# Linear attention, gated MLP and MLP in one launch: side jobs held back during a value product, one low half put out earlier

## The chip, the cores and the metric

The program runs on one core of a Trainium2 chip. The metric is the device time of one execution in microseconds (us). Five engines work side by side: PE multiplies matrices (PEld loads its weights), DVE and POOL do element-wise arithmetic, ACT does activations and copies, SP issues DMAs. POOL issues DMAs too.

## What is computed

```python
def _attn_ref(q, k, v, omega):            # 4 x 8 heads, 576 tokens, head_dim 64, 128 features
    scale = 1.0 / np.sqrt(np.sqrt(D))
    def phi(x):
        h = x @ omega.T - sum(x * x) / 2
        return np.exp(h - max(h)) / np.sqrt(m)
    kv = phi(k).T @ v;  z = sum(phi(k))
    return (phi(q) @ kv) / (phi(q) @ z + 1e-6)

def _moe_ref(x, w_gate, w_val, w_out, rms_g):   # 2304 tokens, d_model 512, d_ff 1536
    xn = x / rms(x) * rms_g
    return (silu(xn @ w_gate) * (xn @ w_val)) @ w_out

def _moe2_ref(x, w_in, w_out):                  # d_ff 2048
    return silu(x @ w_in) @ w_out

out = _moe2_ref(_moe_ref(_attn_ref(q, k, v, omega), ...), ...)
```

(The reference's formulas in short form: phi is applied to scaled q and k, and rms is the root mean square over d_model.) All of it is float32, and the weights reach the kernel as 64-bit numbers.

## The kernel before, in words

**Arithmetic.** A float32 factor is held as two fp32r tiles: a high half (an ACT copy that rounds) and a low half (DVE: the number minus its high half). Each product is three matmul passes: high by high, high by low, low by high (`PASS`). For activations that is `split_h`: L198 on ACT makes "h high", L199 on DVE makes "h low". For weights it is L468 (ACT) and L472 (DVE).

**Tokens.** The 2304 tokens stand in five blocks j = 0 to 4: four of 512 and one of 256. d_model is cut into four pieces d (KC = 4) of 128 rows.

**Weights.** A weight tile of 128 x 512 arrives as two 32-bit words (`raw`). Five DVE instructions (L146 to L157) and two POOL adds (L160) make a float of them ("decoding"); for the gate and value weights ACT scales by the RMS gain (L168, four instructions); then L468 and L472 split.

**Phases.** The first 205 us or so are the attention, with the first two f (pieces of 128 of d_ff) of the gated MLP for blocks 0 to 2 mixed in. Then `stream` sets the order: blocks 3 and 4 of those two f, then the *third f* for all five blocks in the order j = 1, 0, 2, 3, 4. For one block, `g1_glu` multiplies by the gate weights ("g", L205), applies silu (L227), puts the previous block's output products (`mid`, "y", L272, made by `g2_glu`) in between, multiplies by the value weights ("v", L205), multiplies both (DVE, L233) and splits the result into h. `g2_glu` makes y in four pieces d; in the third f these go through staging tiles, copied by ACT (L284) two pieces to a tile, to DRAM by an adding DMA that POOL issues (L288), and a staging tile is only free again when its DMA has landed. In the last GLU step each piece is instead added to ya (DVE, L294), copied to its high half (ACT, L296), and `low(d)` (L262) makes its low half one piece later; `low` of the last piece came after the loop's last yield.

After the third f come GLU units u = 0 to 8, one f each, and then units of the second MLP, two f each. `quad` runs a unit's input product for blocks 0 to 3 with seven products in place of eight; it needs sums and differences of tokens (`token_sums`: L398, L401 on DVE, split by L390 on ACT and L393 on DVE) and of weights (tile `ws`, L367 on POOL, split by L468 and L472; they are the keys ("s", u, 0) and ("s", u, 1), and the jobs `slo(0)` and `slo(1)` make their low halves). In `quad`, L607 are the input products, L619 and L634 ACT's silu and copies, L639 a DVE addition of two partial products, L701 and L715 the DVE products before h is split. `glu_block` (L738, L741) does block 4. In the first MLP unit `mlp_block` and `g1_mlp` work without `quad`.

**What sets the order.** The program is written out by one driver loop. `stream` yields the cost of each piece of PE work, and the loop puts side jobs between them:

```python
        for c in stream():
            due += c
            gone = gone + c if sums or ... else 0.0
            if sums and gone > wq.rest:
                sums.pop(0)()
                gone = ...
            if wq.hold:
                due = min(due, M_PACE)
            elif due > wq.pace and wq.tick():
                due = min(due - wq.pace, wq.pace)
```

`sums` is the list of token-sum jobs, one being written out each `wq.rest` of PE work; `wq.tick` writes out the next weight job (a decoding step, a split, a sum of weights) each `wq.pace`. Where a job stands in an engine's instruction order is therefore where it waits: each engine executes its own list in order.

Of the kernel before, what the change touches and what calls it, by code (L numbers as in the profile page):

```python
# [20 lines left out]
def kernel(  # L21
# [22 lines left out]
    KC = DM // P  # L44
# [177 lines left out]
    def g1_glu(f, j, hs, mid):  # L222
        wq.need((1, "g", f))
        p = ps_tile("ps_g" if blocks[j] == TB * P else "ps_y", [P, blocks[j]])
        yield from proj2(wt[1, "g", f], j, p)
        s = pools["s"][0].tile([P, blocks[j]], F32, tag="s", name="s", bufs=pools["s"][1])
        nc.scalar.activation(out=s, in_=p, func=AF.Silu)  # L227
        if blocks[j] == TB * P:
            yield from mid
        wq.need((1, "v", f))  # L230
        p = ps_tile("ps_g" if blocks[j] == TB * P else "ps_y", [P, blocks[j]])
        yield from proj2(wt[1, "v", f], j, p)
        nc.vector.tensor_tensor(out=s, in0=s, in1=p, op=ALU.mult)  # L233
        if mid is None:
            wait.append(lambda: hs.update({f: split_h(s, j)}))
            return
        hs[f] = split_h(s, j)
        if blocks[j] < TB * P:
            yield from mid
# [15 lines left out]
    def g2_glu(fs, j, hs, first, last, calm=False):  # L255
        wq.need(*[(1, "o", f) for f in fs])
        staged = j < NE and not last
        y = ya[j].rearrange("p (c t) -> p c t", c=KC)
        nn = 3 * len(fs)

        def low(d):
            (nc.gpsimd if 0 < j < NE else nc.vector).tensor_tensor(  # L262
                out=xs[j][:, 1, d, :], in0=y[:, d, :],
                in1=xs[j][:, 0, d, :].bitcast(F32), op=ALU.subtract,
            )

        for d in range(KC):
            ps = ps_tile("ps_y", [P, blocks[j]])
            n = 0
            for f in fs:  # L270
                for a, c in PASS:
                    nc.tensor.matmul(  # L272
                        out=ps,
                        lhsT=wt[1, "o", f][:, a, d * P:(d + 1) * P],
                        rhs=hs[f][:, c, :],
                        start=(n == 0),
                        stop=(n == nn - 1),
                    )
                    n += 1
            if staged:  # L280
                if d % 2 == 0:
                    o = stage()
                if d % 2 == 0 or calm:
                    nc.scalar.activation(out=o[:, d % 2, :], in_=ps, func=AF.Copy)  # L284
                else:
                    nc.vector.tensor_copy(out=o[:, 1, :], in_=ps)
                if d % 2:
                    nc.gpsimd.dma_start(  # L288
                        out=kept(j, d // 2), in_=o.rearrange("p t d -> p (t d)"), accum_op=ALU.add
                    )  # L290
            elif first:
                nc.scalar.activation(out=y[:, d, :], in_=ps, func=AF.Copy)
            else:
                nc.vector.tensor_tensor(out=y[:, d, :], in0=ps, in1=y[:, d, :], op=ALU.add)  # L294
            if last:
                nc.scalar.activation(out=xs[j][:, 0, d, :], in_=y[:, d, :], func=AF.Copy)  # L296
                if d:
                    low(d - 1)
            yield nn * blocks[j] / 2365
        if last:  # L300
            low(KC - 1)

    def out_pair(j, n):
        i = j * TB + 2 * n
# [118 lines left out]

    class WeightQueue:
        def __init__(self):
            self.jobs, self.st, self.hold, self.free, self.held, self.tail, self.pace, self.rest = [], {}, True, [], {}, [], A_PACE, T_PACE
            for u in range(len(groups)):
                self.plan(u)

# [318 lines left out]
        else:  # L748
            wait.append(lambda: hs.update({f: split_h(s, j)}))

    def mlp_block(f, j, hs, ys, n):
        wq.need((2, "i", f))
        p = ps_tile("ps_g", [P, blocks[j]])
        for k in range(2):
            yield 3 * KH * blocks[j] / 2365
            part(wt[2, "i", f], j, p, 3 * KH * k, 3 * KH * (k + 1))
            yield from take(ys, n[k])
        s = pools["s"][0].tile([P, blocks[j]], F32, tag="s", name="s", bufs=pools["s"][1])
        nc.scalar.activation(out=s, in_=p, func=AF.Silu)
        hs[f] = split_h(s, j)  # L760

    def take(ys, n):
        for _ in range(n):
# [4 lines left out]
    def flush():  # L768
        while wait:
            wait.pop(0)()  # L770
        yield from ()
# [5 lines left out]
    def stream():  # L777
# [27 lines left out]
        for n, (j, fs) in enumerate(order):  # L805
# [4 lines left out]
            if n == 1:  # L810
# [2 lines left out]
                    wq.slot(("t", k), F32)  # L813
                now, later23 = sums23()
                sums.extend(now)
                wq.rest = 2.0
            if n == 2:
                sums[:0] = later
                wq.free += [(0, 4), (0, 5)]
# [6 lines left out]
        for u, (kind, fs) in enumerate(groups):  # L826
# [6 lines left out]
            if std <= u < std + NSTD:  # L833
# [7 lines left out]
                for n, k in enumerate(each):  # L841
# [4 lines left out]
                            ys = chain_of(ys, out_of(1))  # L846
                        wq.release(*wq.keys(u - 1)[1])
                    j = 3 - n // 2 if first else 1 - n // 2
                    yield from mlp_block(fs[n % 2], j, hs[j], ys, k if n < 3 else (k[0], 9))
                wq.hold = False  # L850
                if first:
                    assert wq.jobs.pop(0)[0] == 1 << 10
# [762 lines left out]
    with tc.manual_schedule():  # L1615
# [68 lines left out]
        for c in stream():  # L1684
            due += c
            gone = gone + c if sums or wq.rest in (T_PACE, M_PACE + T_PACE) else 0.0
            if sums and gone > wq.rest:
                sums.pop(0)()
                gone = gone - wq.rest if wq.rest not in (T_PACE, M_PACE + T_PACE) else 0.0
# [34 lines left out]
```

## Time and profile before

| | us |
|---|---|
| three runs | 946.83, 951.12, 951.9 (median 951.12) |
| the profiled execution, its own time | 951.37 |
| its span in the profile | 949.6 |
| PE busy | 929.1 (98%) |
| DVE busy | 709.4 (75%) |
| ACT busy | 530.7 (56%) |
| POOL busy | 477.5 (50%) |

The page's chain that ended last is 86% PE, 7% DVE, 3% ACT. A timeline row of one engine gives the start in us from the start of the span, the time it took, engine and line, operation, destination and source, how many instructions it stands for, and in brackets how long the engine sat idle before it and which instruction or DMA ended that. PEclk in the windows is the granted clock of TensorE as a share of full speed.

### The profile page before, as it was taken

The numbers are of one execution on the slowest core, as the hardware profiler recorded it, in microseconds if no ns is written. First come the engines' busy times: TensorE is split into PE (matmuls) and PEld (weight loads), VectorE is DVE, ScalarE is ACT, GpSimd is POOL, SyncE is SP. The second block draws the span as 40 slices with busy tenths as digits, with TensorE's granted clock in tenths as the row PEclk, the third lists the DMA queues.
The fourth block names the chain that finished last, engine by engine and source line by source line (L and its number), as shares of the span: only waits on it lengthen the run. The fifth ranks groups of instructions, "written<-read, shape, count | busy, mean of one in ns | idle before, by whom it ended". The sixth has DMA issues, their size and how long they took to land.

```text
span 949.6 us, 17368 instructions
## 1 busy us (share of the span) xinstructions
PE 929.1 (98%) x6480; PEld 776.0 (82%) x6480; DVE 709.4 (75%) x1323; ACT 530.7 (56%) x1157; POOL 477.5 (50%) x495
## 2 busy tenths in 40 slices
PE   8999999997999999999999999999999999999998
PEld 6888878885878888888888877888888888888886
DVE  6998999866777867877787888978675757575633
ACT  6999977644455355454445445556444454545442
POOL 8888655005435645545454554465554545454411
PEclk9999999999999999999999999999999999999999
DMA  7655543306347658658657740646878787878777
GB/s 187 171 135 146 139 127 101 144 25 143 78 89 158 139 103 181 134 105 180 144 100 156 177 156 3 215 117 136 161 130 170 129 164 136 158 147 148 116 147 166
DMA packets 98788, 129.65 MB, mean 137 GB/s; under 512 B 29456, under 2 KB 75792, under 8 KB 98704
## 3 DMA queue, kind: packets, MB, share of 16 engines
q0 software_dynamic: 17280, 59.78, 36.4%
q1 hardware_dynamic: 81152, 68.70, 25.2%
q8 instruction: 51, 0.84, 0.4%
q14 instruction: 33, 0.27, 0.1%
q10 hardware_dynamic: 272, 0.07, 0.0%
HBM read 54.59 MB, written 69.21 MB: 130 GB/s over the span
## 4 chain that ended last, share of the span: by engine, by line
PE 86%; DVE 7%; ACT 3%; POOL 2%; issue 1%; DMA 1%; SPq 0%; DVEq 0%; ACTq 0%; POOLq 0%
PE g L607 28%; PE y L324 20%; PE y L272 12%; PE y L205 5%; PE g L205 4%; PE b L1192 4%; PE b L205 4%; PE b L1376 2%; PE kv L1272 2%; PE b L1165 2%; PE b L1592 2%; POOL m L160 1%; DVE ya L294 1%; DMA out_dram<-w 1%; PE b L1352 1%
## 5 line engine op out<-in xcount | busy, mean ns | idle before, releaser
L160 POOL TENSOR_TENSOR m<-m,raw 128x512 int32<-128x512 int32 x136 | 203.6, 1498 | 205.8 <-DVE m L157 99.0
L324 PE MATMUL y<-w,h 128*128 128x512 f32 (+1 forms) x870 | 212.2, 388 | 0.6 <-DVE h L199 0.4
L324 PEld LDWEIGHTS y<-w,h 128*128 128x128 f32 x870 | 161.9, 188 | 34.8 <-DVE h L199 0.9
L607 PE MATMUL g<-xs,w 128*128 128x512 f32 x720 | 182.0, 390 | 1.2 <-DVE s L639 1.2
L199 DVE TENSOR_TENSOR h<-s,h 128x512 fp32r<-128x512 f32 (+1 forms) x125 | 95.0, 771 | 97.8 <-ACT h L198 97.7
L272 PE MATMUL y<-h,w 128*128 128x512 f32 (+1 forms) x648 | 152.9, 373 | 8.0 <-ACT h L198 5.2
L607 PEld LDWEIGHTS g<-xs,w 128*128 128x128 f32 x720 | 134.1, 188 | 28.8 <-DVE s L639 1.6
L272 PEld LDWEIGHTS y<-h,w 128*128 128x128 f32 x648 | 116.1, 192 | 32.5 <-ACT h L198 6.0
L349 POOL DMA_DIRECT2D out_dram<-ya x64 | 58.9, 996 | 116.8 <-DVE ya L343 49.4
L198 ACT ACTIVATE h<-s 128x512 fp32r<-128x512 f32 (+1 forms) x125 | 74.0, 597 | 42.7 <-DVE s L233 20.3
L288 POOL DMA_DIRECT2D out_dram<-w x54 | 47.9, 893 | 82.9 <-ACT w L284 78.1
L341 ACT ACTIVATE ya<-y 128x512 f32<-128x512 f32 x82 | 48.3, 594 | 68.7 <-PE y L324 61.3
L205 PE MATMUL g<-xs,w 128*128 128x512 f32 x336 | 80.8, 390 | 2.4 <-DVE xs L262 2.4
L1241 ACT ACTIVATE e<-b,nb 128x128 f32<-128x128 f32 x272 | 75.8, 422 | 7.3 <-issue 4.0
L343 DVE COPY ya<-y 128x512 f32<-128x512 f32 x52 | 35.8, 688 | 58.7 <-PE y L324 58.7
L205 PEld LDWEIGHTS g<-xs,w 128*128 128x128 f32 x336 | 62.5, 188 | 16.0 <-DVE xs L262 3.3
L619 ACT ACTIVATE g<-g 128x512 f32<-128x512 f32 x60 | 34.9, 582 | 68.0 <-PE g L607 67.4
L634 ACT ACTIVATE s<-s 128x512 f32<-128x512 f32 x42 | 26.6, 632 | 81.6 <-DVE s L639 81.6
L472 DVE TENSOR_TENSOR w<-m,w 128x512 fp32r<-128x512 f32 x74 | 69.7, 942 | 1.3 <-ACT w L468 1.3
L607 PE MATMUL g<-w,w 128*128 128x512 f32 x270 | 69.0, 391 | 0.4 <-DVE s L639 0.4
L607 PE MATMUL g<-ya,w 128*128 128x512 f32 x270 | 68.5, 389 | 0.0
L205 PEld LDWEIGHTS y<-xs,w 128*128 128x128 f32 x480 | 60.1, 188 | 2.0
(138 smaller groups left out, 1585.7 us busy)
## 6 DMA issues: line engine op xcount, KB each, us to landing
out_dram<-w POOLq DMA_DIRECT2D x56, 512.0 KB, 7.0
out_dram<-ya POOLq DMA_DIRECT2D x52, 512.0 KB, 6.9
raw<-in_moe_w_out_dram SPq DMA_DIRECT2D x28, 512.0 KB, 4.5
raw<-in_moe_w_in_dram SPq DMA_DIRECT2D x16, 512.0 KB, 4.6
out_dram<-ya SPq DMA_DIRECT2D x14, 512.0 KB, 4.7
raw<-in_moe_w_gate_dram SPq DMA_DIRECT2D x12, 512.0 KB, 4.1
raw<-in_moe_w_val_dram SPq DMA_DIRECT2D x12, 512.0 KB, 4.5
qT<-e SPq DMA_DIRECT2D x72, 64.0 KB, 2.4
```

The source lines that it names most:

```text
L160: tt(out=mi, in0=mi, in1=(low if step == 5 else high).bitcast(I32), op=ALU.add)
L198: nc.scalar.activation(out=ht[:, 0, :], in_=s, func=AF.Copy)
L199: nc.vector.tensor_tensor(out=ht[:, 1, :], in0=s, in1=ht[:, 0, :].bitcast(F32), op=ALU.subtract)
L205: nc.tensor.matmul(out=ps, lhsT=w[:, a, cc * P:(cc + 1) * P], rhs=xs[j][:, c, cc, :], start=(n == 0), stop=(n == 3 * KC - 1),)
L272: nc.tensor.matmul(out=ps, lhsT=wt[1, "o", f][:, a, d * P:(d + 1) * P], rhs=hs[f][:, c, :], start=(n == 0), stop=(n == nn - 1),)
L288: nc.gpsimd.dma_start(out=kept(j, d // 2), in_=o.rearrange("p t d -> p (t d)"), accum_op=ALU.add)
L324: nc.tensor.matmul(out=ps, lhsT=hs[f][:, a, t * P:(t + 1) * P], rhs=wt[2, "p", f][:, c, d0:d1], start=(n == 0), stop=(n == nn - 1),)
L341: nc.scalar.activation(out=o[:, t % 2, :], in_=ps, func=AF.Copy)
L349: nc.gpsimd.dma_start(out=rows, in_=o[p0:p1], accum_op=ALU.add)
L472: eng.tensor_tensor(out=v[:, 1, :], in0=x, in1=v[:, 0, :].bitcast(F32), op=ALU.subtract)
L607: nc.tensor.matmul(out=ps, lhsT=w[:, a, (c0 + c) * P:(c0 + c + 1) * P], rhs=x(b, c), start=(start and n == 0), stop=(n == 3 * KH - 1), ski ...
L1241: nc.scalar.activation(out=st.e[r][:, :, h, :] if blocks4 else st.e[r][:, h, :], in_=src.rearrange("p (a f) -> p a f", a=4) if blocks4 els ...
```

## The change

- **Held back** (`calm`): while a value product of the third f is being written out, the driver loop runs no side jobs, neither token sums nor weight jobs; their counters go on.
- **Paces**: the weight jobs' first pace goes from 1.8 (`A_PACE`) to 2.4, until unit 0 sets it anew; the token sums' rest in the third f goes from 2.0 to 1.8.
- **Last low half**: `low(3)` of the last GLU step is written with the last piece's high half, before the yield, and not after it.
- **First MLP pair**: `mlp_block` puts the split of h on the `wait` list, to be flushed after the next half product, where it was written at once.

```diff
 def g1_glu
+        wq.calm = f == sweeps[1][1][0]
         yield from proj2(wt[1, "v", f], j, p)
+        wq.calm = False
         nc.vector.tensor_tensor(out=s, in0=s, in1=p, op=ALU.mult)
 def g2_glu
                 if d:
                     low(d - 1)
+                if d == KC - 1:
+                    low(d)
             yield nn * blocks[j] / 2365
-        if last:
-            low(KC - 1)
 class WeightQueue
-            self.jobs, ..., self.pace, self.rest = ..., A_PACE, T_PACE
+            self.jobs, ..., self.pace, self.rest = ..., 2.4, T_PACE
+            self.calm = False
 def mlp_block
             part(wt[2, "i", f], j, p, 3 * KH * k, 3 * KH * (k + 1))
+            yield from flush()
             yield from take(ys, n[k])
...
-        hs[f] = split_h(s, j)
+        if put_off:
+            wait.append(lambda: hs.update({f: split_h(s, j)}))
+        else:
+            hs[f] = split_h(s, j)
 def stream
-                wq.rest = 2.0
+                wq.rest = 1.8
...
-                    yield from mlp_block(fs[n % 2], j, hs[j], ys, k if n < 3 else (k[0], 9))
+                    yield from mlp_block(fs[n % 2], j, hs[j], ys, k if n < 3 else (k[0], 9), first)
+                yield from flush()
 driver loop
             gone = gone + c if sums or wq.rest in (T_PACE, M_PACE + T_PACE) else 0.0
+            if wq.calm:
+                continue
             if sums and gone > wq.rest:
```

The lists of PE and SP are the same before and after; those of DVE, ACT and POOL differ in the third f, in the GLU units, and at the end of the last GLU unit. The code after L233 stands two lines further down in the changed kernel (L233 is L235, L284 is L286, L294 is L296, L398 is L400, L401 is L403), and three from `WeightQueue` on (L472 is L475, L639 is L642). The held-back splits of `mlp_block` alone change no engine's list: what it would move is written out again at the same place.

DVE in the third f, from the token sums before block 0's product s (L233) to block 2's. Before:

```order
L398 TENSOR_TENSOR ya_96<-xs_92 128x1024
L401 TENSOR_TENSOR ya_96<-ya_96 128x1024
L146 TENSOR_SCALAR m_4013<-raw_3962 128x512
L149 TENSOR_SCALAR raw_3962<-raw_3962 128x512
L152 TENSOR_SCALAR m_4013<-m_4013 128x512
L154 TENSOR_SCALAR raw_3962<-raw_3962 128x512
L157 TENSOR_SCALAR m_4013<-m_4013 128x512
L233 TENSOR_TENSOR s<-s,g 128x512
L199 TENSOR_TENSOR h<-s,h 128x512
L401 TENSOR_TENSOR ya_96<-ya_96,w_1_3923 128x1024
L472 TENSOR_TENSOR w_4_4039<-m_3964,w_4_4039 128x512
L393 TENSOR_TENSOR ya_4047<-ya_96,ya_4047 128x1024
L393 TENSOR_TENSOR ya_4075<-ya_96,ya_4075 128x1024
L472 TENSOR_TENSOR w_5_4081<-m_4013,w_5_4081 128x512
L233 TENSOR_TENSOR s<-s,g 128x512
```

With the change:

```order
L403 TENSOR_TENSOR w_1_3915<-ya_96,w_1_3915 128x1024
L400 TENSOR_TENSOR ya_96<-xs_92 128x1024
L403 TENSOR_TENSOR ya_96<-ya_96 128x1024
L235 TENSOR_TENSOR s<-s,g 128x512
L199 TENSOR_TENSOR h<-s,h 128x512
L403 TENSOR_TENSOR ya_96<-ya_96,w_1_3915 128x1024
L146 TENSOR_SCALAR m_4033<-raw_3961 128x512
L149 TENSOR_SCALAR raw_3961<-raw_3961 128x512
L152 TENSOR_SCALAR m_4033<-m_4033 128x512
L154 TENSOR_SCALAR raw_3961<-raw_3961 128x512
L157 TENSOR_SCALAR m_4033<-m_4033 128x512
L395 TENSOR_TENSOR ya_4031<-ya_96,ya_4031 128x1024
L395 TENSOR_TENSOR ya_4057<-ya_96,ya_4057 128x1024
L235 TENSOR_TENSOR s<-s,g 128x512
```

The second decoding (L146 to L157) stands behind block 0's product now and not ahead of it; ahead of block 2's product (the last row of each) no low half of a weight (L472, now L475) is left.

ACT in the same place, from the copies of block 1's y to h high of block 2 (the second L198; rows with m are scalings, with w_4 and w_5 high halves of weights, with w_2 and w_3 copies to staging tiles). Before:

```order
L284 ACTIVATE w_2_3951<-y 128x512 x2
L284 ACTIVATE w_3_3952<-y 128x512 x2
L198 ACTIVATE h<-s 128x512
L168 ACTIVATE m_3964<-m_3964,g_sb 128x128 x4
L468 ACTIVATE w_4_4039<-m_3964 128x512
L390 ACTIVATE ya_4047<-ya_96 128x1024
L227 ACTIVATE s<-g 128x512
L284 ACTIVATE w_2_3951<-y 128x512 x2
L284 ACTIVATE w_3_3952<-y 128x512
L390 ACTIVATE ya_4075<-ya_96 128x1024
L168 ACTIVATE m_4013<-m_4013,g_sb 128x128 x4
L468 ACTIVATE w_5_4081<-m_4013 128x512
L284 ACTIVATE w_3_3952<-y 128x512
L198 ACTIVATE h<-s 128x512
```

With the change:

```order
L286 ACTIVATE w_2_3950<-y 128x512 x2
L286 ACTIVATE w_3_3951<-y 128x512 x2
L198 ACTIVATE h<-s 128x512
L392 ACTIVATE ya_4031<-ya_96 128x1024
L227 ACTIVATE s<-g 128x512
L286 ACTIVATE w_2_3950<-y 128x512
L392 ACTIVATE ya_4057<-ya_96 128x1024
L286 ACTIVATE w_2_3950<-y 128x512
L168 ACTIVATE m_3963<-m_3963,g_sb 128x128 x4
L471 ACTIVATE w_4_4069<-m_3963 128x512
L286 ACTIVATE w_3_3951<-y 128x512 x2
L198 ACTIVATE h<-s 128x512
```

The second weight's four scalings and its high half are gone from ahead of h high of block 2, and the first weight's stand behind two copies of block 0's y.

DVE at the start of GLU unit 2, from the last h of the unit before to the low half of its first weight sum, `slo(0)` (the row with ws; w_4 is the gate weight). Before:

```order
L701 TENSOR_TENSOR s<-s 128x512
L199 TENSOR_TENSOR h<-s,h 128x512
L715 TENSOR_TENSOR s<-s,g 128x512
L738 TENSOR_TENSOR both<-both,y 128x256
L199 TENSOR_TENSOR h<-s,h 128x512
L294 TENSOR_TENSOR ya_3688<-y,ya_3688 128x512 x3
L472 TENSOR_TENSOR w_2_5143<-ws,w_2_5143 128x512
```

With the change:

```order
L704 TENSOR_TENSOR s<-s 128x512
L199 TENSOR_TENSOR h<-s,h 128x512
L718 TENSOR_TENSOR s<-s,g 128x512
L741 TENSOR_TENSOR both<-both,y 128x256
L199 TENSOR_TENSOR h<-s,h 128x512
L475 TENSOR_TENSOR w_4_5068<-m_4987,w_4_5068 128x512
L296 TENSOR_TENSOR ya_3688<-y,ya_3688 128x512 x4
L475 TENSOR_TENSOR w_2_5153<-ws,w_2_5153 128x512
```

The low half of the gate weight, which stood some rows earlier before, and a fourth addition to ya stand ahead of `slo(0)` now. The starts of units 1 to 8 are alike in this.

## Rows read from the trace of the kernel before

**Rows 1.** Busy time by windows: PE, PEld, DVE, ACT, POOL, clock, DMA share, GB/s.

```profile
205.00:264.00 59.00, 51.33 (x226) 41.04 (x224) 41.85 (x62) 24.83 (x46) 25.29 (x19) 0.94 0.46 97
264.00:545.00 281.00, 281.00 (x1375) 237.97 (x1376) 218.83 (x395) 141.96 (x289) 138.64 (x130) 1.00 0.67 138
545.00:585.00 40.00, 35.68 (x167) 28.28 (x166) 31.11 (x52) 19.84 (x37) 17.21 (x12) 1.00 0.28 101
```

**Rows 2.** Timeline of PE, third f: start, us, operation, idle before and releaser.

```profile
221.41 0.50 PE L272 MATMUL y<-h,w 128*128 128x512 f32 x1 [1.99 <-ACT h L198]
222.35 4.36 PE L272 MATMUL y<-h,w 128*128 128x512 f32 x11 [0.44 <-DVE h L199]
226.55 5.60 PE L205 MATMUL g<-xs,w 128*128 128x512 f32 x24
...
236.25 4.35 PE L272 MATMUL y<-h,w 128*128 128x512 f32 x11 [0.40 <-DVE h L199]
```

**Rows 3.** Windows as in rows 1, two stretches with a lower clock.

```profile
222.50:226.00 3.50, 3.50 (x9) 2.75 (x10) 3.50 (x3) 2.08 (x4) 0.95 (x1) 0.51 1.04 198
236.20:239.70 3.50, 3.45 (x8) 2.78 (x9) 3.31 (x2) 1.20 (x2) 3.50 (x3) 0.51 0.74 126
```

**Rows 4.** Timeline of DVE, third f.

```profile
213.80 1.22 DVE L398 TENSOR_TENSOR ya<-xs 128x1024 f32<-128x1024 f32 x1
215.05 2.21 DVE L401 TENSOR_TENSOR ya<-ya 128x1024 f32<-128x1024 f32 x1
...
220.02 0.67 DVE L233 TENSOR_TENSOR s<-s,g 128x512 f32<-128x512 f32 x1
...
233.96 0.68 DVE L233 TENSOR_TENSOR s<-s,g 128x512 f32<-128x512 f32 x1
...
243.44 0.69 DVE L233 TENSOR_TENSOR s<-s,g 128x512 f32<-128x512 f32 x1 [3.90 <-PE g L205]
```

**Rows 5.** Timeline of POOL, third f.

```profile
213.96 4.46 POOL L160 TENSOR_TENSOR m<-m,raw 128x512 int32<-128x512 int32 x2 [38.49 <-DVE m L157]
```

**Rows 6.** Timeline of ACT, third f.

```profile
226.03 1.09 ACT L284 ACTIVATE w<-y 128x512 f32<-128x512 f32 x2 [1.41 <-PE y L272]
...
230.37 1.05 ACT L390 ACTIVATE ya<-ya 128x1024 fp32r<-128x1024 f32 x1
231.32 1.26 ACT L168 ACTIVATE m<-m,g_sb 128x128 f32<-128x128 f32 x4
...
234.67 0.63 ACT L198 ACTIVATE h<-s 128x512 fp32r<-128x512 f32 x1 [0.94 <-DVE s L233]
```

**Rows 7.** Chain that ended last, 205 to 300 us.

```profile
219.17 10.34 DMA out_dram<-w
```

**Rows 8.** DMAs of the stages, 205 to 262 us, from the tile's view.

```profile
DMA to landing us min/median/max: 5.1/6.2/10.3
```

**Rows 9.** Timeline of PE, GLU unit 0.

```profile
259.76 1.66 PE L607 MATMUL g<-w,w 128*128 128x512 f32 x6 [0.39 <-DVE s L639]
...
263.93 0.50 PE L607 MATMUL g<-xs,w 128*128 128x512 f32 x1 [1.15 <-DVE s L639]
```

**Rows 10.** Timeline of DVE, start of GLU unit 1.

```profile
279.01 0.69 DVE L199 TENSOR_TENSOR h<-s,h 128x512 fp32r<-128x512 f32 x1 [0.37 <-ACT h L198]
279.62 1.88 DVE L294 TENSOR_TENSOR ya<-y,ya 128x512 f32<-128x512 f32 x3
281.41 0.68 DVE L472 TENSOR_TENSOR w<-ws,w 128x512 fp32r<-128x512 f32 x1
...
284.29 1.48 DVE L472 TENSOR_TENSOR w<-m,w 128x512 fp32r<-128x512 f32 x1
```

**Rows 11.** Timeline of PE, start of GLU unit 1.

```profile
282.57 1.52 PE L607 MATMUL g<-xs,w 128*128 128x512 f32 x6
```

**Rows 12.** Timeline of PE, last GLU unit.

```profile
558.12 0.73 PE L205 MATMUL g<-xs,w 128*128 128x512 f32 x2 [2.19 <-DVE xs L262]
```

**Rows 13.** Timeline of DVE, last GLU unit.

```profile
558.58 0.42 DVE L738 TENSOR_TENSOR both<-both,y 128x256 f32<-128x256 f32 x1
```

More of the change, by code (lines that the diff above doesn't have):

```diff
@@ L425, in __init__ @@
         def __init__(self):
-            self.jobs, self.st, self.hold, self.free, self.held, self.tail, self.pace, self.rest = [], {}, True, [], {}, [], A_PACE, T_PACE
+            self.jobs, self.st, self.hold, self.free, self.held, self.tail, self.pace, self.rest = [], {}, True, [], {}, [], 2.4, T_PACE
+            self.calm = False
             for u in range(len(groups)):
@@ L749, in glu_block, with mlp_block @@
             wait.append(lambda: hs.update({f: split_h(s, j)}))
-    def mlp_block(f, j, hs, ys, n):
+    def mlp_block(f, j, hs, ys, n, put_off):
         wq.need((2, "i", f))
```

## The prediction

> **What bounds the kernel now.** I read the windows first [rows 1]. Over the 281 us of most of the GLU units PE is busy all the time at full clock, so there nothing can be won, only lost. In the 59 us of the third f PE lacks 7.67 us (59.00 less 51.33), at a mean clock of 0.94; in the 40 us around the last GLU step it lacks 4.32 us. These two windows hold everything that the change could win.
>
> The PE timeline of the third f shows where [rows 2]. PE waits twice for an h of the third f: 1.99 us for the high and 0.44 us for the low half of block 0's, and then for block 2's, whose low half releases the second product at 236.25. Behind each wait the eleven products that follow run at a granted clock of 0.51, the 1.2 GHz level [rows 3]. From 222.35 to the next group at 226.55 they take 4.20 us. The 24 products of that group take 5.60, or 0.233 each, so eleven would take 2.57 at full clock: a slow stretch costs 1.6 us.
>
> Why is h late? On DVE, block 0's product s stood behind a token difference, a sum that took 2.21 us beside POOL's adds, and a decoding; it starts at 220.02 [rows 4, 5]. Block 2's s starts only at 233.96, behind the low half of a weight (the order lists show it), and that waits for ACT: a token half at 230.37, four scalings at 231.32 and the weight's high half [rows 4, 6]. All of this followed a staging DMA that took 10.34 us on the chain [rows 7] and so landed at 219.17 + 10.34 = 229.51.
>
> **The change part by part.**
>
> *Block 0's wait.* DVE now has a sum (L403), a difference (L400) and another sum ahead of s. With 2.21 us for each of the sums beside POOL and 1.25 for the difference [rows 4] that is 5.67 us from 213.80, 219.47 against 220.02. Without POOL in the way it is about 3.8; but POOL's adds span 213.96 to 218.42 [rows 5], so I take the contended end, and, rounding down, **0.4 us**. This wait stays, and I let its slow stretch stay.
>
> *Block 2's wait.* No weight's low half stands ahead of s, so DVE can multiply when PE has made v, and h high is up to ACT. ACT has, from its copy at 226.03 on: copy 0.55 (half of 1.09), token half 0.95 (230.37 to 231.32), copy 0.55, four scalings 1.26, a high half 0.6 (like the 0.63 of an h high of the same size), two copies 1.09: together 5.0, so h high starts at 231.03 [rows 6]. From h high at 234.67 to the second product at 236.25 it took 1.58 [rows 2, 6], which puts that product at 232.61: 3.64 us earlier. The last two copies need the staging tile whose DMA landed at 229.51; they are due at 229.94, so it is just in time. PE's group of g and v, which began at 226.55, ends 5.60 later and 0.4 earlier than before, at 231.75: the idle time shrinks to 0.9 us. The idle 2.19 us before 558.12 [rows 12] left the clock at 1.00 [rows 1], so I take the slow stretch as gone, 1.6 more. Together **5.2 us** (the 0.4 is in it, since ACT sets the end), bounds 0 (DMA late, below) and 6.4. What was moved out of the way, two low halves of weights at 0.61, a token half (1.2, like the difference of the same size at 213.80) and a product of block 4 (0.4, like L738 [rows 13]), falls behind it and before unit 0's first weight sum: 2.8 us, into the 3.90 us that DVE idled before block 3's product [rows 4].
>
> What would undo that is the clock. The Trainium skill, page "TensorE: Matmul & The Clock Gate", section "What's actually happening", says that the chip's watch on PE's activity runs freely and is not tied to the kernel's start. By it the same idle time may cost the clock in one execution and not in another. The trace bears out half of that: 2.43 us of waiting lost the clock at 222.35, 2.19 us at 558.12 did not.
>
> *Unit 0.* PE waits there for two sums of partial products, 0.39 and 1.15 us [rows 9]. In the new DVE list the first stands ahead of the decoding that was ahead of it, and the second has five decoding steps less ahead. Both waits should go, less a remnant: **1.3 us** (0.4 to 1.54).
>
> *Starts of units 1 to 8.* This is the cost. The slower pace of weight jobs shifts all later ones. In DVE's list the gate weight's low half (which had stood before the last additions of the unit ahead) and the fourth addition to ya now stand between h low and `slo(0)`. Before, `slo(0)` began at 281.41 and was done at 282.09 (0.68 later). PE's second product with it begins at 282.57 [rows 11], and its third instruction, the first that reads the low half, at 282.57 + 2 x 0.233 = 283.04: a margin of 0.95. What is put ahead takes 0.61 for the low half (as from 279.01 to 279.62, same size) and 0.60 for the addition (three from 279.62 to 281.41) [rows 10]: 1.21. That is 0.26 over the margin, 0.3 with the hop from one engine to the other, and eight starts lose **2.4 us** (bounds: 0 if something ahead of h low also gets shorter by 0.3, 15 by the rival below). The gate weight's low half is no longer due earlier, so nothing else is gained by its moving. PE does not wait anywhere else in this window now [rows 1], and the queues of PE and SP are written in the same order as before; POOL's adds for one decoding slide past a staging DMA, which already waits for ACT's copies.
>
> *Last low half.* PE waits 2.19 us for it [rows 12]. Written a step earlier it is done before 556, and two products can go. But the y product that follows fills a PSUM buffer that block 4's `both` (L738) frees, at 558.58 + 0.42 = 559.00 [rows 13]. That is late next: `low` now stands ahead of the chain (L639, L634, L701, L198, L715) that leads to L738, and no longer inside it, so L738 keeps its time. The y group started 0.58 after 558.12, and its first three products are not held by that buffer; the fourth would now start at about 559.05, against 558.70 + 3 x 0.233 = 559.40. I take **0.3 us**; the bound is 2.19, if the buffer is freed by something else.
>
> *The put-off splits* of the first MLP pair move no instruction on any engine, by the order lists: 0. That part of the change does nothing.
>
> *Sum.* 5.2 + 1.3 + 0.3 - 2.4 = 4.4 us less. The profiled execution took 951.37 us by its own time, 1.77 over its span, and stands 0.25 over the median of the three runs (951.12). 951.37 - 4.4 = **947.0 us**.
>
> **The rivals.**
>
> *No cost at the unit starts.* h low, or the additions before it, come 0.3 us earlier, since the gate weight's low half leaves the DVE list ahead of h. For it: only 0.3 is lacking. Against: h low waited for ACT's h high, 0.37 us [rows 10], so DVE was not its limit. Time: 951.37 - 6.8 = 944.6.
>
> *The slow stretch stays* behind block 2's wait: 3.6 instead of 5.2, so 948.6. For it: the shorter of the two clock losses followed 2.43 us of waiting, and 0.9 is still a wait; against: 2.19 us without a loss.
>
> *The staging DMA is late for the first copy.* Of the stages' DMAs the middle one took 6.2 us, the longest 10.3 [rows 8]. If it is the first of the pair that takes as long as the second did, ACT's 5.0 us begin at about 229.9, h high starts at 234.9 and the product at 236.4: nothing won there, and 951.37 + 0.8 = 952.2. For it: one of six took that long. The Trainium skill, page "DMA: Bandwidth & Descriptors", section "Anatomy of one DMA — SWDGE (gpsimd) path", gives about 2.0 us plus the bytes at 436 GB/s. For the 512 KB of a stage that is 3.2 us, an estimate by that page; by it this rival has no chance. The rows, 6.2 in the middle, speak against the estimate here.
>
> *Slower: the unit starts lose far more.* Beside POOL's adds the same low half took 1.48 us at 284.29, and 0.68 at 281.41 [rows 10]. If both low halves ahead of PE's third instruction now meet POOL, each start loses 0.30 + 2 x 0.8 = 1.9, eight lose 15.2, and the time is 951.37 - 6.8 + 15.2 = 959.8; if only one does, 1.1 each, 953.4. It decides from 0.85 us a start on (all gains eaten), and passes 0.5% from 1.44 on. For it: POOL is busy 138.64 us of these 281 [rows 1]. Against: at that moment nothing slowed `slo(0)` before, and the sums on POOL have to end before it.
>
> **How the numbers follow.** 0.5% is 4.75 us, about what a measurement of this kernel can tell from no change; 946.4 and 955.9 are the bounds. The forecast gets 0.40, of which 0.12 lies below 946.4, since its own bounds (944.6 to 949) cross that line; no cost at the starts 0.22 (faster); the slow stretch stays 0.12 (same); the late DMA 0.14 (same); more lost at the starts 0.12, half with one low half met (same), half with both (slower). Faster 0.34, same 0.60, slower 0.06. The range 943.5 to 953.0 leaves out the worst of the last rival and a tail at each end.
>
> **What would show it.** In the changed kernel's PE timeline: block 2's y, second product, near 232.6 with about 0.9 us of idle time before it and no window at 0.5 behind it; in unit 0 no wait for L642; eight waits of about 0.3 us for L475, each at the third instruction of a unit's second product, in a window that had none; the wait for `low` replaced by one of 1 to 2 us for L741 on DVE. If PE still waits for block 2 until 235 or later, the DMA or the ACT list is misread; if the GLU window is idle by over 7 us, the contention is.

## The result and the profile after

The changed kernel takes 961.53 us (median of 6 runs, 959.39 to 963.42) against 950.72 us for the kernel before (6 runs): 1.0113 times as long, 95% interval 1.0088 to 1.0138. It is slower by some 10.8 us. The forecast was 4.4 us less, 947.0, and a range that ended at 953.0.

The span in the profile went from 949.6 to 960.1 us. The first two windows of [rows 1], of the changed kernel (PE, PEld, DVE, ACT, POOL, clock, DMA share, GB/s):

```profile
205.00:264.00 59.00, 53.68 (x244) 43.62 (x243) 37.95 (x61) 27.16 (x51) 22.97 (x18) 0.94 0.44 90
264.00:545.00 281.00, 275.13 (x1323) 227.85 (x1322) 219.26 (x377) 135.70 (x276) 138.71 (x126) 1.00 0.64 131
```

Beside [rows 1], the third f's window lacks 5.32 us of PE instead of 7.67, so something was won there; but the GLU window, full before, now lacks 5.87 us. A busy share doesn't give the whole loss, because the row of a PE group runs on into the start of the next one, and so hides part of a wait. A ledger does: in each GLU unit PE runs block 4's 24 products ("y<-xs,w" of L205, 128x256) once, and the time between two such groups is a unit's period. PE's timeline of the changed kernel, with the groups and the waits of two units:

```profile
309.14 2.99 PE L205 MATMUL y<-xs,w 128*128 128x256 f32 x24
...
313.27 2.79 PE L274 MATMUL y<-h,w 128*128 128x512 f32 x11 [0.68 <-DVE h L199]
...
318.85 1.21 PE L610 MATMUL g<-xs,w 128*128 128x512 f32 x4 [0.30 <-DVE w L475]
...
345.24 2.99 PE L205 MATMUL y<-xs,w 128*128 128x256 f32 x24
...
417.20 2.99 PE L205 MATMUL y<-xs,w 128*128 128x256 f32 x24
...
425.89 1.19 PE L610 MATMUL g<-xs,w 128*128 128x512 f32 x4 [0.31 <-DVE w L475]
...
452.25 2.99 PE L205 MATMUL y<-xs,w 128*128 128x256 f32 x24
```

In the kernel before, the first of these groups, and the products with h that follow it without a wait, stand here:

```profile
309.21 2.99 PE L205 MATMUL y<-xs,w 128*128 128x256 f32 x24
312.04 2.92 PE L272 MATMUL y<-h,w 128*128 128x512 f32 x12
```

The next group there is at 343.47, 34.26 later. Now it is 36.10 in a unit with both waits and 35.05 in one with the second alone. Here is the whole ledger, from the starts of these groups in the two profiled executions:

| stage | before | after | difference |
|---|---|---|---|
| to block 4's products of the second f (just ahead of the third f) | 197.17 | 198.20 | +1.03 |
| third f, to block 4's products in it | 46.00 | 44.16 | -1.84 |
| unit 0 | 31.77 | 30.65 | -1.12 |
| seven periods, units 1 to 7 | 239.87 | 250.25 | +10.38 |
| unit 8, to the first MLP pair | 34.59 | 37.65 | +3.06 |
| from there to the end | 400.2 | 399.2 | -1.0 |

The sum is 10.5, the spans' difference. The first row is no effect of the change (its lists there are the same; more on it at the end). The second row is from one execution of each kernel: with the same lists, the runs below have 43.1 to 44.2 us there for the change, and 44.8 and 46.0 for the kernel before. So the change won 4.0 us where it was meant to act and lost 13.4 in units 1 to 8, which it was not about.

**What happens at the start of a unit.** First the changed kernel's DVE at the start of unit 2, with block 4's group at 309.14:

```profile
309.49 1.89 DVE L704 TENSOR_TENSOR s<-s 128x512 f32<-128x512 f32 x1 [0.70 <-ACT s L637]
312.07 1.14 DVE L199 TENSOR_TENSOR h<-s,h 128x512 fp32r<-128x512 f32 x1 [0.70 <-ACT h L198]
...
315.12 0.69 DVE L475 TENSOR_TENSOR w<-m,w 128x512 fp32r<-128x512 f32 x1
315.72 2.48 DVE L296 TENSOR_TENSOR ya<-y,ya 128x512 f32<-128x512 f32 x4
318.11 0.68 DVE L475 TENSOR_TENSOR w<-ws,w 128x512 fp32r<-128x512 f32 x1
```

The same kernel's POOL:

```profile
309.18 0.86 POOL L290 DMA_DIRECT2D out_dram<-w  x1 [0.77 <-ACT w L286]
309.75 1.07 POOL L369 TENSOR_TENSOR ws<-m 128x256 f32<-128x256 f32 x1
310.89 1.08 POOL L369 TENSOR_TENSOR ws<-ws,m 128x256 f32<-128x256 f32 x1
```

In the kernel before, DVE's first two rows and POOL's first sum were:

```profile
309.44 0.69 DVE L701 TENSOR_TENSOR s<-s 128x512 f32<-128x512 f32 x1 [0.70 <-ACT s L634]
310.83 1.15 DVE L199 TENSOR_TENSOR h<-s,h 128x512 fp32r<-128x512 f32 x1 [0.70 <-ACT h L198]
308.48 1.07 POOL L367 TENSOR_TENSOR ws<-m 128x256 f32<-128x256 f32 x1
```

The changed kernel's ACT:

```profile
305.98 0.59 ACT L286 ACTIVATE w<-y 128x512 f32<-128x512 f32 x1
306.46 1.27 ACT L168 ACTIVATE m<-m,g_sb 128x128 f32<-128x128 f32 x4
307.77 0.63 ACT L471 ACTIVATE w<-m 128x512 fp32r<-128x512 f32 x1
308.30 0.58 ACT L286 ACTIVATE w<-y 128x512 f32<-128x512 f32 x1
```

Read the changed kernel's from the last to the first. ACT puts four scalings and a high half between two copies to staging tiles; before, the copies stood together, 1.07 us from 305.56. So POOL issues the second copy's DMA late, and its four sums of weights, which stand behind it, begin at 309.75 where they began at 308.48. Just before, at 309.49, DVE starts the product L704. In the kernel before (L701, at 309.44) it took 0.69, now 1.89: it ends at 311.38, 0.56 after the first sum. That spacing is the same wherever the two meet: in 95 of the 96 unit starts of the twelve profiled executions the product ends 0.55 to 0.60 us after the first sum's end, whatever its own start. So where the sum is late, the product is late. ACT's high half and L199 follow it, h low ends at 313.21, and PE starts its second product at 313.27. Before, L199 began at 310.83, took 1.15 and ended at 311.98. PE's group began at 312.04, and its second product, the first that reads h low, followed 0.23 later, at 312.27: there was a margin of 0.29. Now the group begins at 312.09, and the second product comes not at 312.32 but at 313.27. The wait for h low is the first loss.

The second is the one that the prediction costed: in DVE's list L475 and a fourth L296 stand ahead of the first weight sum's low half, which ends at 318.79, and PE waits for it at 318.85. The row says 0.30, but PE's two products before it start at 317.93 and take 0.23 each (24 in 5.60 [rows 2]), so PE in fact stood from 318.39 to 318.85. A unit with this wait alone lasts 35.05, 0.78 longer than 34.27. Not all of that is the two rows ahead of the low half: POOL's sums are late in those units too, by 0.31, and L704 takes 0.97 there, which moves everything behind it by 0.28. The Trainium skill, page "SBUF — State Buffer", section "Who interferes with whom", says that DVE instructions with two SBUF inputs contend with POOL instructions that read SBUF, and its section "Terms" that the loser is blocked for the whole instruction. L704 agrees with this: 1.89 - 0.69 = 1.20, about one sum on POOL (1.07). Which of the two is held, the rows don't settle: here it is L704, whose row starts 0.26 ahead of the sum's, and in the one exception (unit 8 of the run with holding back alone) L704 keeps its 0.69 with a sum that starts 0.25 behind it.

**The third f.** PE's timeline there, answering to [rows 2]:

```profile
220.75 0.50 PE L274 MATMUL y<-h,w 128*128 128x512 f32 x1 [0.30 <-ACT h L198]
221.48 2.79 PE L274 MATMUL y<-h,w 128*128 128x512 f32 x11 [0.22 <-DVE h L199]
224.10 5.60 PE L205 MATMUL g<-xs,w 128*128 128x512 f32 x24
233.73 5.79 PE L274 MATMUL y<-h,w 128*128 128x512 f32 x12 [4.02 <-ACT h L198]
```

The two stretches behind block 0's and block 2's waits (columns as in the windows above):

```profile
222.50:226.00 3.50, 3.50 (x17) 2.90 (x16) 2.87 (x7) 0.00 (x0) 1.74 (x2) 1.00 0.98 228
233.70:237.20 3.50, 3.47 (x8) 2.46 (x9) 3.49 (x5) 3.05 (x8) 0.61 (x1) 0.50 1.08 178
```

Block 0's wait is nearly gone and its slow stretch with it. Block 2's is longer, 4.02 us, and its slow stretch is there. In the kernel before it was 3.20 for h high and then 0.40 [rows 2]:

```profile
235.35 0.50 PE L272 MATMUL y<-h,w 128*128 128x512 f32 x1 [3.20 <-ACT h L198]
```

Why, the changed kernel's POOL and ACT show. POOL:

```profile
215.00 5.60 POOL L160 TENSOR_TENSOR m<-m,raw 128x512 int32<-128x512 int32 x2 [38.49 <-DVE m L157]
220.54 2.02 POOL L290 DMA_DIRECT2D out_dram<-w  x2
```

ACT:

```profile
228.33 0.60 ACT L286 ACTIVATE w<-y 128x512 f32<-128x512 f32 x1 [6.20 <-DMA out_dram<-w]
228.83 1.05 ACT L392 ACTIVATE ya<-ya 128x1024 fp32r<-128x1024 f32 x1
229.78 0.59 ACT L286 ACTIVATE w<-y 128x512 f32<-128x512 f32 x1
230.25 1.27 ACT L168 ACTIVATE m<-m,g_sb 128x128 f32<-128x128 f32 x4
231.55 0.63 ACT L471 ACTIVATE w<-m 128x512 fp32r<-128x512 f32 x1
232.09 1.06 ACT L286 ACTIVATE w<-y 128x512 f32<-128x512 f32 x2
233.04 0.63 ACT L198 ACTIVATE h<-s 128x512 fp32r<-128x512 f32 x1
```

ACT needs 233.04 - 228.33 = 4.7 us from its first copy to h high (5.0 were reckoned), but the copy waits 6.20 us for a staging tile whose DMA POOL could only issue after its adds of the first decoding, 5.60 us beside DVE's token sums. PE, some 3.5 us earlier than before because block 0's wait and its slow stretch are gone (224.10, less the 1.03 of the later start, against 226.55), has nothing to do meanwhile. In sum, block 0's part (to 224.10, before 226.55) is 3.48 us shorter, and the rest of the third f 1.64 longer, 18.26 against 16.62.

### The profile page after: what moved, and what is told of

Same layout as the page of the kernel before. It is cut to its first block, busy times and chain, and to the rows that moved or that the text cites. A ratio compares the mean times of both kernels' runs of the same rounds, so it can differ in the third digit from the quotient of the medians.

```text
span 960.1 us, 17368 instructions
## 1 busy us (share of the span) xinstructions
PE 934.2 (97%) x6480; PEld 775.6 (81%) x6480; DVE 714.5 (74%) x1323; ACT 531.0 (55%) x1157; POOL 480.1 (50%) x495
## 4 chain that ended last, share of the span: by engine, by line
PE 70%; DVE 15%; ACT 7%; issue 3%; POOL 2%; DMA 2%; SPq 1%; DVEq 0%; ACTq 0%; POOLq 0%
PE g L610 22%; PE y L326 20%; PE y L274 8%; PE g L205 4%; PE b L1200 3%; PE y L205 3%; DVE ya L296 3%; ACT h L198 2%; DVE s L704 2%; DVE h L199 2%; PE b L205 2%; POOL m L160 2%; PE b L1600 2%; PE kv L1280 2%; PE b L1384 2%
## 5 line engine op out<-in xcount | busy, mean ns | idle before, releaser
L160 POOL TENSOR_TENSOR m<-m,raw 128x512 int32<-128x512 int32 x136 | 208.3, 1532 | 227.3 <-DVE m L157 115.3
L199 DVE TENSOR_TENSOR h<-s,h 128x512 fp32r<-128x512 f32 (+1 forms) x125 | 101.5, 823 | 75.9 <-ACT h L198 75.7
L198 ACT ACTIVATE h<-s 128x512 fp32r<-128x512 f32 (+1 forms) x125 | 74.2, 598 | 57.8 <-DVE s L704 22.8
L205 PE MATMUL g<-xs,w 128*128 128x512 f32 x336 | 80.7, 391 | 0.0
L205 PEld LDWEIGHTS g<-xs,w 128*128 128x128 f32 x336 | 63.0, 189 | 13.1
L475 DVE TENSOR_TENSOR w<-m,w 128x512 fp32r<-128x512 f32 x74 | 66.5, 899 | 9.0 <-ACT w L471 9.0
L205 PEld LDWEIGHTS y<-xs,w 128*128 128x128 f32 x480 | 60.2, 188 | 2.1
L205 PE MATMUL y<-xs,w 128*128 128x256 f32 x480 | 60.8, 280 | 0.0
```

The costliest lines, as they stand in the source:

```text
L160: tt(out=mi, in0=mi, in1=(low if step == 5 else high).bitcast(I32), op=ALU.add)
L198: nc.scalar.activation(out=ht[:, 0, :], in_=s, func=AF.Copy)
L199: nc.vector.tensor_tensor(out=ht[:, 1, :], in0=s, in1=ht[:, 0, :].bitcast(F32), op=ALU.subtract)
L205: nc.tensor.matmul(out=ps, lhsT=w[:, a, cc * P:(cc + 1) * P], rhs=xs[j][:, c, cc, :], start=(n == 0), stop=(n == 3 * KC - 1),)
L475: eng.tensor_tensor(out=v[:, 1, :], in0=x, in1=v[:, 0, :].bitcast(F32), op=ALU.subtract)
```

## The experiments

Each ran beside the kernel before on the same chip; times are medians, with the ratio to that kernel and its 95% interval. Theory A: the weight jobs stand one job behind from unit 0 on, and it is their new places in units 1 to 8 that cost, through the two waits above.

**Holding back alone**, in the kernel before. By the order of the lists, holding back alone shifts the units' weight jobs as the change does; the first pace alone and the rest alone don't; both paces together do.

```diff
 def g1_glu
+        wq.calm = f == sweeps[1][1][0]
         yield from proj2(wt[1, "v", f], j, p)
+        wq.calm = False
 driver loop
+            if wq.calm:
+                continue
             if sums and gone > wq.rest:
```

> The kernel before with the holding back during value products of the third f alone; both paces as before. The lists of DVE, ACT and POOL from unit 1 on are then those of the change, though no pace was altered. Theory A (the change's loss is in the place of the weight jobs in units 1 to 8, wherever the shift came from): unit periods of 35.0 to 36.1 us instead of 34.27, the same waits of 0.3 us for L472's and 0.67 us for L199's successors at each unit's start, 957 to 962 us. Theory B (the slower first pace of 2.4 makes weights late): no loss in the units, 947 to 951 us.

Measured: 961.88 us against 951.25, ratio 1.0109 (1.0096 to 1.0123). The periods of units 1 to 7 are 36.11, 35.59, 36.05, 36.00, 35.00, 35.03 and 34.77, unit 8 lasts 37.78, and the waits are the same two. The slower pace is not needed for the loss.

**The first pace put back.**

```diff
-self.jobs, ..., self.pace, self.rest = ..., 2.4, T_PACE
+self.jobs, ..., self.pace, self.rest = ..., A_PACE, T_PACE
```

> The change with the weight jobs' first pace put back to 1.8; holding back, rest 1.8 and the early last low half stay. The lists of DVE, ACT and POOL in the units are those of the kernel before, those of the third f nearly those of the change up to block 2's product. Theory A: no wait at the unit starts, period 34.27, and what the third f (1.8 us), unit 0 (1.1) and the last low half (1.0) gave stays: 945 to 949 us. Rival: holding side jobs back costs by itself, since they must be caught up with in the units: 955 or more.

Measured: 950.32 against 951.25, ratio 0.9991 (0.9978 to 1.0004). No wait in the units, all periods 34.27; so holding back need not be paid for there. (Apart from the last low half, this run differs from the one with holding back alone by the rest of 1.8 in place of 2.0: it is the counters together that set the places.) But the gain is smaller than expected: unit 0's two waits (0.42 and 1.16) are back with the old places, block 2's wait is 4.79, and the interval takes in no change.

**The last low half alone.**

```diff
                 if d:
                     low(d - 1)
+                if d == KC - 1:
+                    low(d)
             yield nn * blocks[j] / 2365
-        if last:
-            low(KC - 1)
```

> The kernel before with the last low half of the last unit's tokens written out with its step, nothing else. Theory A: PE's wait of 2.19 us for it goes, waits for L741 and L738 (block 4's buffers) of about 0.9 and 0.4 us come in its place: 0.3 to 1.0 us less, 949.7 to 950.7 against 951. Rival: the wait was the whole price, 2.2 us less. Second rival: the buffer re-forms all of it, no change.

Measured: 950.84 against 951.25, ratio 0.9986 (0.9973 to 1.0000): 0.4 us less, and the interval runs from nothing to 2.6. PE's timeline of this run shows the wait that takes the old one's place:

```profile
558.22 0.96 PE L272 MATMUL y<-h,w 128*128 128x512 f32 x3 [1.18 <-ACT both L741]
559.61 0.96 PE L272 MATMUL y<-h,w 128*128 128x512 f32 x3 [0.42 <-DVE both L738]
```

1.60 of the 2.19 us are re-formed at once, as predicted, by block 4's buffers; the first of them, ACT's L741, was not named.

**The first repair: the weight sum's low half one job earlier.**

```diff
-                    (1, lambda: shi(0)),
-                    (0, lambda: slo(0), lambda: dec(bs[0], 0), ...),
+                    (1, lambda: shi(0), lambda: slo(0)),
+                    (0, lambda: dec(bs[0], 0), ...),
```

> The change, with the low half of the first weight sum put out one job earlier in the GLU units, so that in DVE's list it stands ahead of the fourth addition to ya and not behind it. Theory A (two separate costs: a wait of 0.73 us of PE time per unit start for this low half, in all eight, and in five of them another 1.05 for an h low half that POOL's sums delay): the first goes, the second stays: unit periods 34.3 and 35.3, 5 to 6 us less than the change, 955 to 957 us. Rival (the sums themselves come late, so that the low half waits for ACT's high half wherever it stands): no gain, 960 to 962.

Measured: 955.36 against 951.25, ratio 1.0042 (1.0028 to 1.0056); 6.2 less than the change's 961.53. The seven periods sum to 244.1 instead of 250.25. No wait for L475 is left in units 1 to 8, and those for h low stay, in four units, between 0.22 and 0.68. Unit 5, which had this wait alone, lasts 34.27 and not 35.05. That 0.78 isn't yet the price of the low half's place, for L704 is back at 0.69 there as well. Unit 8 lasts 38.90 in this run, 1.25 more than with the change.

**The second repair: the value weight's scalings one job earlier.** DVE's, POOL's and PE's lists are those of the change.

```diff
                     (0, lambda: dec(a0, 0), lambda: load(u, bs[0], 0)),
-                    (0,),
-                    (1, lambda: hi(a1)),
+                    (0, lambda: w_scale(st[a1])),
+                    (1, lambda: hi(a1, False)),
```

> The change with the four scalings of the value weight put out one job earlier in the GLU units; the lists of DVE, POOL and PE stay those of the change. ACT then reaches the copy to the second staging tile 1.3 us earlier, POOL's DMA and the four sums behind it start 1.3 us earlier, as in the kernel before. Theory A: L704 takes 0.7 and not 1.9 us, PE's wait of 0.67 us for the h low half (1.05 with what it drags along) goes in the five units that had it, the wait for the first weight sum's low half stays in all: 956 us, within 954.5 to 958. Rival (h is late by DVE's own queue and POOL has no part in it): no change, 960 to 962.

Measured: 954.08 against 951.15, ratio 1.0037 (1.0022 to 1.0053); 7.5 less than the change. POOL's sums and DVE's product at the start of unit 2 now stand as in the kernel before. POOL in this run:

```profile
305.49 1.08 POOL L369 TENSOR_TENSOR ws<-m 128x256 f32<-128x256 f32 x1
```

DVE in this run:

```profile
306.45 0.69 DVE L704 TENSOR_TENSOR s<-s 128x512 f32<-128x512 f32 x1 [0.70 <-ACT s L637]
307.84 1.15 DVE L199 TENSOR_TENSOR h<-s,h 128x512 fp32r<-128x512 f32 x1 [0.70 <-ACT h L198]
```

L704 takes 0.69 where it begins as the first sum on POOL ends, and 1.89 where the sum begins right after it. PE waits for no h low in the units; the waits for L475 stay in all of them, 0.17 to 0.30. The seven periods sum to 243.61, 6.64 less than the change's 250.25: that is about what POOL's late sums cost, through h low and through the low half of the weight sum. Where L704 is at 0.69 (units 2, 3 and 5) the period is 34.73 or 34.74. So the place of L475 alone costs 0.47 us a unit, with 0.17 in PE's row. It gained 2 us more than expected: the wait for L475 became shorter too.

**Both repairs.**

> The change with both: the first weight sum's low half one job earlier and the value weight's scalings one job earlier. Theory A (the two costs are separate and make up the loss in units 1 to 7): periods near 34.3, only the 3 us of the last unit left over: 950 to 952.5 us. Rival (they are one cost, and each repair alone takes all of it): no better than the better of the two alone, about 955.

Measured: 951.31 against 951.15, ratio 1.0000 (0.9987 to 1.0012); 10.2 less than the change. The seven periods are 34.42 and six times 34.27. So the two waits make up the loss of units 1 to 7, 10.38 us. They are not quite separate: the repairs alone took 6.15 and 6.64 off the seven periods, together 10.21, since L704's delay is in both waits. Unit 8 still lasts 37.46, and that is what eats the gains.

**One job ahead.**

```diff
             wq.std = u < std + NSTD
+            for _ in range(1 if u == 1 else 0):
+                wq.tick()
```

> The change with one more weight job written out at the start of unit 1, nothing else. From unit 2 on the lists of DVE, ACT and POOL are then those of the kernel before again, apart from the last low half. Theory A (the change's loss is that the queue of weight jobs is one job behind in the units): the periods go back to 34.27 and unit 8 loses its 3.1 us more than before; what the third f, unit 0 and the last low half gave stays. From the stages of the two traces, the change lost 13.4 us from unit 1 to the first MLP unit, so 961.5 - 13.4 = 948, within 946 to 950. Rival (the loss hangs on the third f, which still hands everything over later): periods over 35, 956 or more.

Measured: 949.68 against 951.15, ratio 0.9977 (0.9966 to 0.9988). Units 2 to 7 last 34.27 again and unit 8 34.58; unit 1, whose start comes too soon for the extra job, still lasts 36.07. One job's place in the queue is what 13.4 us hung on, unit 8's 3 us included. What waits in unit 8 is seen in the changed kernel's ACT and PE. ACT:

```profile
552.10 0.63 ACT L471 ACTIVATE w<-m 128x512 fp32r<-128x512 f32 x1 [1.25 <-POOL m L160]
552.64 0.58 ACT L622 ACTIVATE g<-g 128x512 f32<-128x512 f32 x1
```

PE:

```profile
553.27 1.65 PE L610 MATMUL g<-w,w 128*128 128x512 f32 x6 [0.24 <-ACT g L622]
...
559.42 1.66 PE L610 MATMUL g<-w,w 128*128 128x512 f32 x6 [1.75 <-DVE s L642]
```

A weight's high half waits for POOL's decoding, with silu's copy and h behind it on ACT. From that h's low half on DVE (L199 at 553.80) to L642 (558.68) it is 4.88 us, and was 4.90 in the kernel before, so the delay is handed on to PE's second wait. That this is the whole of the 1.75 us was not tried by itself.

**Outputs held back too.** As the run before, and in the third f also during the output products:

```diff
         if blocks[j] == TB * P:
+            wq.calm = f == sweeps[1][1][0]
             yield from mid
```

> As the run with one more job at unit 1, and side jobs are also held back during the third f's output products, so that POOL's second decoding stands behind all four staging DMAs of blocks 1 and 0. If PE's wait of 4 us for block 2's h hangs on the second decoding on POOL or DVE, it shrinks and the time is 945 to 947. If it hangs on the first staging DMA, which POOL issues only after the first decoding, it stays and the time is that of the run with one more job, 947 to 950.

Measured: 949.41 against 951.15, ratio 0.9982 (0.9973 to 0.9992). The time is that of the run with one more job, yet for another reason than expected: the third f drops to 37.49 us, 8.5 less than before, with one wait of 0.99 us and the clock at 1.00 behind it. POOL in this run:

```profile
214.09 2.70 POOL L160 TENSOR_TENSOR m<-m,raw 128x512 int32<-128x512 int32 x2 [38.48 <-DVE m L157]
216.73 2.00 POOL L291 DMA_DIRECT2D out_dram<-w  x2
```

Without DVE's token sums beside them, the two adds take 2.70 us and not 5.60, and the first staging DMAs go out earlier. ACT, too, has only copies ahead of block 2's h high in this run. But unit 0 then waits for its own weights (2.65 us for L476 the longest) and lasts 36.97, 5.2 more than before, and unit 1 keeps its 1.8.

**Two more versions.** Like the two runs just before, they beat both kernels. The extra job at unit 1, with both repairs in unit 1 alone, and the third f as in the change:

> The change with one more weight job at unit 1 and both repairs in unit 1 alone; third f as in the change. Theory A: the run with one more job lost 1.8 us in unit 1 still; that goes: 949.7 - 1.8 = 948, within 946.5 to 949. Rival: the loss of unit 1 is handed on to unit 2 (its weights late): 949.5 to 951.

Measured: 948.08 against 951.01, ratio 0.9971 (0.9960 to 0.9983). Unit 1 lasts 34.45 and hands nothing on.

The same, with side jobs also held back during the output products that are written out with block 0 of the third f:

```diff
+            wq.calm = f == sweeps[1][1][0] and j in (0,)
             yield from mid
+            wq.calm = False
```

> The change with one more weight job at unit 1, both repairs (first sum's low half and value weight's scalings one job earlier) in unit 1 alone, and side jobs also held back during the output products that are written out with block 0 of the third f, so that the second decoding stands behind block 0's product on DVE and behind three staging DMAs on POOL. Theory A: nothing is lost in units 1 to 8 (all periods 34.27), unit 0 keeps at least half of its 1.1 us, the last low half gives 1.0, and the wait of 4 us for block 2's h shrinks below 2 with no fall of the clock behind it, since ACT has no scaling ahead of that h: 942 to 946 us. Rival: as with the outputs all held back, unit 0 pays for its late weights what the third f wins: 948 to 950.

Measured: 947.80 against 951.01, ratio 0.9968 (0.9955 to 0.9981), which is not to be told from the other. The third f lasts 42.50 and units 1 to 7 34.26 to 34.41, but unit 0 lasts 31.39, with 0.38 of its 1.12 us of gain left, and the wait for block 2's h did not shrink; it is 4.20. ACT in this run:

```profile
228.37 0.60 ACT L288 ACTIVATE w<-y 128x512 f32<-128x512 f32 x1 [1.48 <-DMA out_dram<-w]
228.87 1.05 ACT L394 ACTIVATE ya<-ya 128x1024 fp32r<-128x1024 f32 x1
...
232.44 0.63 ACT L198 ACTIVATE h<-s 128x512 fp32r<-128x512 f32 x1 [1.10 <-DVE s L237]
```

DVE in this run:

```profile
229.95 1.87 DVE L397 TENSOR_TENSOR ya<-ya,ya 128x1024 fp32r<-128x1024 f32 x1 [3.25 <-ACT ya L394]
```

The scalings are gone from ahead of h high, but two token halves moved into their place, behind the same staging DMAs, and the first one's low half (L397) stands ahead of block 2's product s on DVE, for which h high waits. POOL's adds (2.68 us) and the first staging DMAs (from 217.93) are as early here as in the run with the outputs held back too, so they alone don't shorten the wait. The expectation of a wait below 2 us was wrong.

## Why the prediction was wrong

- **Starts of units 1 to 8: wrong, and it decided the sign.** The step that the gate weight's low half and a fourth addition stand ahead of `slo(0)` held (waits of 0.30 to 0.33 in the rows, 0.3 forecast). But it was mis-sized. The price of this place alone is 0.47 a unit, as the run with the scalings earlier shows, so eight starts would cost some 3.8 us and not 2.4; with L704's delay on top, a unit with this wait alone lasts 0.78 longer. The shift was put down to the slower pace; holding back alone makes it as well.
- **What was left out: h low.** This weighs most: bringing POOL's sums back takes 6.64 of the 10.38 us off units 1 to 7. The prediction said that PE waits nowhere else in this window, since it had not before. It did not ask how much room h low had. In the kernel before it ended 0.29 us ahead of the product that reads it. ACT's list at this place, with the scalings between two copies, was not followed on to POOL's DMA and the sums behind it. That is some 1 us in each of five unit starts. The rival on the slower side had the right mechanism, DVE held up beside POOL's adds, but at the wrong instruction: the two low halves kept 0.69 and 0.68, and the product L704 met the sums. It was given 0.12.
- **Unit 8: left out too**, 3.06 us.
- **Block 0's wait: more than predicted.** With an offset of 1.03 us for the start, s began 1.7 us earlier, not 0.4: of the two sums ahead of it only one got longer beside POOL's adds (1.22 and 2.21 us).
- **Block 2's wait: wrong.** 5.2 us were forecast. Of ACT's chain the length was right (4.7 against 5.0), its start was not: it was taken from the copy at 226.03, and that copy now waits for a DMA, as in the rival of the late DMA. That DMA took 7.68 us on the chain that ended last, less than the 10.34 of [rows 7]: POOL issued it later, and PE came earlier. That rival was right that nothing is won at this wait. All of the third f gave 1.84 us, and that came from block 0.
- **The clock.** The slow stretch behind block 2's wait was taken as gone because 0.9 us of waiting was forecast; it was 4.02, and the granted clock was 0.50 behind it, the 1.2 GHz level. Block 0's stretch, which was to stay, went: 1.00.
- **Unit 0: right in size, wrong in detail.** The two waits for L642 went (1.54 us), a new one for a weight's low half came (0.77 in the row): 1.12 net against 1.3.
- **Last low half: about right**, 0.3 forecast; in the traces, the time from the first MLP pair to the end is 400.2 before, 400.2 with the low half alone, 399.2 with the change.
- **Put-off splits: right**; they move nothing.

## What to carry to other kernels

Where one queue hands out side jobs at a pace, a change to a single stage moves the jobs of all later ones: before costing the stage, lay the lists of the stages behind it side by side and ask, for every producer that PE needs there, by how much it is early now. A margin of 0.29 us isn't seen in a busy table that reads 100%. And cost a new wait by the period it lengthens, not by the idle time in its row (0.17 in the row was 0.47 in the period).

## What the runs showed of the hardware

The same wait may or may not cost the clock. In the run with the last low half alone, the third f's lists are those of the kernel before and block 0's wait is the same, 2.00 and 0.44 us. PE's timeline of that run:

```profile
223.11 0.50 PE L272 MATMUL y<-h,w 128*128 128x512 f32 x1 [2.00 <-ACT h L198]
224.06 2.79 PE L272 MATMUL y<-h,w 128*128 128x512 f32 x11 [0.44 <-DVE h L199]
```

The eleven products take 2.79 us here, at a granted clock of 1.00 (223.90 to 227.40), and took 4.36 before, at 0.51 [rows 2, 3]. That agrees with the Trainium skill, page "TensorE: Matmul & The Clock Gate", section "What's actually happening", by which the watch on PE's activity is not tied to the kernel's start. Whether the clock falls makes 1.6 us of scatter at this place from run to run that no change to the kernel explains.

The start scatters as well. In the twelve profiled executions, PE reaches block 4's products of the second f between 195.87 and 199.64 us, with the same lists up to there. A difference of 1 us between two spans says nothing before this is taken off.
